# One kernel, its instruction groups issued in the order of a stored table instead of a greedy list

## The chip, the core and the metric

The kernel runs on one core of one Trainium2 chip. The core has a matrix engine (TensorE, "PE" in the profile; "PEld" is its loading of weights), VectorE (DVE), ScalarE (ACT), GpSimd (POOL), and SyncE (SP), which here issues all DMA transfers. Each engine works through its own list of instructions in order, and waits on semaphores for the others. The metric is the device time of one execution in microseconds.

## What is computed

A gated linear attention, whose state decays by alpha and takes in the product of k and v at each of 768 steps, for 4 batches of 8 heads of width 48. Its output, as a matrix of 768 by 384 for each batch, goes through a low-rank mix over the sequence and an MLP of width 1536 with a ReLU:

```python
def _attn_ref(q, k, v, alpha):
    B, H, S, D = q.shape                      # 4, 8, 768, 48
    state = np.zeros((B, H, D, D))
    for t in range(S):
        state = alpha[:, :, t, :, None] * state + np.einsum('bhd,bhe->bhde', k[:, :, t], v[:, :, t])
        y[:, :, t] = np.einsum('bhd,bhde->bhe', q[:, :, t], state)
    return y

def _moe_ref(x, U, V, w_ch1, w_ch2):          # x: (4, 768, 384)
    xt = x.transpose(0, 2, 1)
    h = xt @ U @ V                            # U: (768, 32), V: (32, 768)
    u = x + h.transpose(0, 2, 1)
    ch = np.maximum(u @ w_ch1, 0.0) @ w_ch2   # (384, 1536), (1536, 384)
    return u + ch
```

## The kernel before

The program is built from **groups**: a few instructions of one engine that are issued together, such as the four transposes of one tile. Each group is added to a plan with the tiles it reads and writes, the engines that may do it with an estimated cost in ns on each, a priority, and a mode (the tile shape that its matmuls use on TensorE: F is the full array; Q, R, C, V are others). A greedy list scheduler, run when the program is built, then orders them: again and again it takes the group that can start first by its estimates, with the priority to break ties, and gives it an engine and a buffer. What it decides is only an order for each engine and a choice of buffers; on the chip the semaphores decide when things run.

```python
class Plan:
    LAT = {"PE": 215.0, "ACT": 155.0, "DVE": 145.0, "POOL": 110.0, "SP": 200.0}
    SWITCH = 95.0
    TOL = 150.0
    EASE = 200.0
    STAY = 20.0
    # ...
    def run(self):
        # ... "ready" holds the groups whose inputs are planned
        while todo:
            per = {}
            for op in ready:
                t = op.est
                # ... t: not before a buffer is free (s[b.reserve])
                at = {eng: max(t, clock.get(eng, 0.0)) for eng in op.engs}
                soon = min(at[eng] + c for eng, c in op.engs.items()) + self.TOL
                for eng, c in op.engs.items():
                    if at[eng] + c <= soon:
                        per.setdefault(eng, []).append((at[eng], op))
            best = None
            for eng, ok in per.items():
                t0 = min(t for t, _ in ok)
                t1, op = min(((t, o) for t, o in ok if t <= t0 + 1.0), key=lambda x: (x[1].prio + (self.STAY if eng == "PE" and x[1].mode != mode else 0.0), x[1].i))
                key = (t1, t1 + op.engs[eng])
                if best is None or key < best[0]:
                    best = (key, eng, op)
            # ... takes a slot of each pool, moves the clocks of the engine and of the DMA
            done = end + self.LAT[eng]
            for b in op.bufs:
                b.left -= 1
                b.last = max(b.last, done + self.EASE)
                if b.left == 0:
                    b.pool.free[b.idx] = b.last
            for u in op.users:
                u.n -= 1
                if eng == "PE" and "PE" in u.engs:
                    u.est = max(u.est, end)
                else:
                    u.est = max(u.est, done + u.slack)
```

The constants that the groups need are made first, on VectorE and GpSimd, before the plan:

```python
    filler = const.tile([128, 512], BF16, name="filler")
    nc.vector.memset(filler, 0.0)
    # ... ones, onesel, offd: small, by memsets on VectorE
    for x in lt_s + rk_s:
        nc.vector.memset(x[:, :, D:], 0.0)
    rv2_s = slots("rw", 4, [C, 2, HP, 2, D], BF16)
    for x in rv2_s[:2]:
        nc.vector.memset(x, 0.0)
    ut_ones = const.tile([C, C], BF16, name="ut_ones")
    make_upper_triangular(nc, ut_ones, val=1.0, diag=True)
    ident = const.tile([C, C], BF16, name="ident")
    make_identity(nc, ident)
    upto = const.tile([C, C], BF16, name="upto")
    nc.vector.tensor_copy(upto, ut_ones)
    nc.vector.memset(upto[0:64, 64:128], 0.0)
    below = const.tile([C, C], BF16, name="below")
    nc.vector.tensor_tensor(below, upto, ident, op=ALU.subtract)
    mask2 = const.tile([C, 2, 2 * C], BF16, name="mask2")
    nc.gpsimd.memset(mask2, 0.0)
    nc.gpsimd.affine_select(
        out=mask2, in_=mask2, compare_op=ALU.is_gt, fill=1.0, base=0, pattern=[[1, 2], [-1, 2 * C]], channel_multiplier=2
    )
    maskp = const.tile([C, 1, 2, C], BF16, name="maskp")
    nc.vector.tensor_copy(maskp[0:64, 0], mask2[0:64, :, 0:C])
    nc.vector.tensor_copy(maskp[64:128, 0], mask2[64:128, :, C : 2 * C])
    maskc = const.tile([C, 1, C], BF16, name="maskc")
    for x in rq_s:
        nc.gpsimd.memset(x[:, :, D:], 0.0)
    for x in rv2_s[2:]:
        nc.gpsimd.memset(x, 0.0)
    nc.gpsimd.tensor_copy(maskc[:, 0, :], ut_ones)
    for g in range(4):
        nc.gpsimd.tensor_copy(sel[:, g, :], ident[0:R, 0:R])
```

The attention is done in units. Batches 0 and 1 have six units each: one is half of the heads over 256 steps, with two chunks of 64 in the halves of the partitions (`stage_pair`); batches 2 and 3 have units of all heads over 128 steps (`stage_gla`). A unit of the first kind, its groups in the order in which they are added (cut):

```python
        P.add({"ACT": 435}, lambda e: nc.scalar.activation(jh(lt()[:, :, 0:D]), raw(at), AF.Ln), r=[at], w=[lt], prio=pr + 40, slack=sl)
        # two groups: rv, v as bf16; POOL or ACT
        def f_cum(e):
            l2 = jh(lt()[:, :, 0:D])
            nc.tensor.matmul(cb()[:, 0:DM].rearrange("p (i h d) -> p i h d", i=2, d=D), lhsT=upto, rhs=l2[:, 0:1].to_broadcast([C, 2, HP, D]), start=True, stop=False)
            nc.tensor.matmul(cb()[:, 0:Q], lhsT=below, rhs=l2[:, 1], start=False, stop=False)
            nc.tensor.matmul(cb()[:, Q : 2 * Q], lhsT=upto, rhs=l2[:, 1], start=False, stop=False)
            # ... the unit's total decay: four narrow matmuls
        P.add({"PE": mm(DM, Q, Q, 8, 4, 4, 4, 4)}, f_cum, r=[lt], w=[cb], prio=pr + 30, slack=sl)
        aa, ai, tot = Buf(aas), Buf(ais), Buf(tots)
        P.add({"ACT": 390}, lambda e: nc.scalar.activation(ai().rearrange("t h d -> t (h d)"), cb()[:, 0:DM], AF.Exp, scale=-1.0), r=[cb], w=[ai], prio=pr + 20, slack=sl)
        P.add({"ACT": 390}, lambda e: nc.scalar.activation(aa().rearrange("t h d -> t (h d)"), cb()[:, 0:DM], AF.Exp), r=[cb], w=[aa], prio=pr + 21, slack=sl)
        P.add({"ACT": 100}, lambda e: nc.scalar.activation(tot()[:, :, 0], cb()[:, DM : DM + 8], AF.Exp), r=[cb], w=[tot], prio=pr + 22, slack=sl)
        both = {"DVE": 420, "POOL": 885}
        P.add(both, lambda e: f_scale(e, rk, kt, ai), r=[kt, ai], w=[rk], prio=pr + 10, slack=sl)
        P.add(both, lambda e: f_scale(e, rq, qt, aa), r=[qt, aa], w=[rq], prio=pr + 11, slack=sl)
        P.add({"PE": mm(*[C] * 4)}, lambda e: f_tr(rk, tk), r=[rk], w=[tk], prio=pr + 18, slack=sl)
        P.add({"PE": mm(*[C] * 4)}, lambda e: f_tr(rq, tq), r=[rq], w=[tq], prio=pr + 18, slack=sl)
        P.add({"DVE": 335, "ACT": 500}, lambda e: f_ev(e, kT, tk, False), r=[tk], w=[kT], prio=pr + 8, slack=sl)
        P.add({"DVE": 600, "ACT": 500}, lambda e: f_ev(e, qT, tq, True), r=[tq], w=[qT], prio=pr + 8, slack=sl)
        def f_sc(e):
            for n in range(4):
                a, j = n // 2, n % 2
                for par in range(2):
                    o = 64 * par
                    for c in range(2):
                        r = slice(64 * c, 64 * c + 64)
                        nc.tensor.matmul(
                            sc[par]()[r, n * C : (n + 1) * C],
                            lhsT=kT()[o : o + D, n, r], rhs=qT()[o : o + D, 2 * a + c, :],
                            start=(n == 0), stop=(n == 3), skip_group_check=True,
                        )

        P.add({"PE": mm(*[C] * 4)}, f_sc, r=[kT, qT], w=[sc[0], sc[1]], prio=pr + 10, mode="Q", slack=sl)
        def f_mask(par):
            s2 = sc[par]().rearrange("p (a j c) -> p a j c", a=2, j=2)
            dst = pm()[:, :, par, :].rearrange("p (a j) c -> p a j c", j=2)
            nc.vector.tensor_tensor(dst, s2, maskp.to_broadcast([C, 2, 2, C]), op=ALU.mult)

        for par in range(2):
            P.add({"DVE": 605}, lambda e, par=par: f_mask(par), r=[sc[par]], w=[(pm, par)], prio=pr + 5, slack=sl)
        # f_d (PE): k times v of the unit; f_st (DVE or POOL): the state, decayed; two chunks
        P.add({"PE": mm(*[2 * D] * 12)}, f_y, r=[qT, (rv, 0), (rv, 1), (pm, 0), (pm, 1)] + [x for x in before if x is not None], w=[yb], prio=pr, slack=sl)
        P.add(
            {"ACT": 385, "DVE": 460},
            lambda e: copy(e, xb()[:, 2 * blk : 2 * blk + 2, half * Q : (half + 1) * Q], yb()[:, 0 : 2 * Q].rearrange("p (c x) -> p c x", c=2)),
            r=[yb], w=[(xb, 2 * blk, half), (xb, 2 * blk + 1, half)], prio=pr, slack=sl,
        )
```

After the six units of a batch the low-rank mix needs all of them (`stage_mix`: utx, its copy, X and H matmuls into uT, copies on ScalarE or VectorE). Then come the two MLP layers, in two halves of the sequence and 12 blocks, and in six blocks of rows:

```python
    def mlp1(b, uT, h1, tt):
        for jt in range(NJ):
            hb = Buf(bank, RES[b])
            pr = mlp_prio(b, 0.25 * tt + jt * 0.02)
            # ...
            def f(e, jt=jt, hb=hb):
                for ct in range(NCT):
                    nc.tensor.matmul(
                        hb()[:, 0:TW], lhsT=w1_sb[:, ct, jt * 128 : (jt + 1) * 128],
                        rhs=uT()[:, ct, tt * TW : (tt + 1) * TW], start=(ct == 0), stop=(ct == NCT - 1),
                    )

            P.add({"PE": mm(TW, TW, TW)}, f, r=need + [("w1", jt // 3, ct) for ct in range(NCT)], w=[hb], prio=pr)
            # ... g: Relu on ScalarE, or max with 0 on VectorE
            P.add({"ACT": 395, "DVE": 470}, g, r=[hb], w=[(h1, tt, jt)], prio=-100)

    def mlp2(b, xb, ub, utx, h1, c):
        hb = Buf(bank, RES[b])
        tt = c // NT
        for g in range(3):   # four matmuls each, over 12 blocks of the hidden layer
            # ...
        ou = Buf(outs)
        P.add({"DVE": 468}, lambda e: nc.vector.tensor_tensor(ou(), (xb if b in XT else ub)()[:, c, :], hb()[:, 0:DM], op=ALU.add), r=[hb] + (xk(b, xb, c) if b in XT else [(ub, c)]), w=[ou], prio=-100)
        P.add({"SP": 550.0}, lambda e: nc.sync.dma_start(out[b, c * C : (c + 1) * C, :], ou()), r=[ou], prio=-1)
```

Where the plan leaves TensorE idle in the first 28 us, filler matmuls on a spare PSUM bank are put in[...].

Of the kernel before, what the change touches and what calls it, by code (L numbers as in the profile page):

```python
# [21 lines left out]
class Buf:  # L22


    def __init__(self, pool, reserve=0):
        self.pool = pool
        self.reserve = reserve
        self.slot = None
        self.idx = 0
        self.left = 0  # L30
        self.last = 0.0
# [5 lines left out]
class Op:  # L37
    __slots__ = ("engs", "fn", "prio", "deps", "bufs", "n", "users", "est", "i", "mode", "slack", "eng", "t")


class Plan:


    LAT = {"PE": 215.0, "ACT": 155.0, "DVE": 145.0, "POOL": 110.0, "SP": 200.0}
    SWITCH = 95.0
    TOL = 150.0
    EASE = 200.0
    STAY = 20.0
# [10 lines left out]
    def add(self, engs, fn, r=(), w=(), prio=0.0, mode="F", slack=0.0, after=()):  # L59
        op = Op()  # L60
        op.engs, op.fn, op.prio, op.mode, op.slack = engs, fn, prio, mode, slack
        op.i = len(self.ops)
        op.deps, op.users, op.est = set(), [], 0.0
# [14 lines left out]
        op.deps.update(x for x in after if x is not None)  # L78
# [12 lines left out]
    def run(self):  # L91
        for op in self.ops:
            op.n = len(op.deps)
            for d in op.deps:
                d.users.append(op)
        ready = [op for op in self.ops if op.n == 0]
        clock = {}
        order = []
        dma = 0.0
        mode = "F"  # L100
        todo = len(self.ops)
        while todo:
            per = {}
            for op in ready:
                t = op.est
                for b in op.bufs:
                    if b.slot is None:
                        s = sorted(x for x in b.pool.free if x is not None)
                        if len(s) <= b.reserve:
                            t = None  # L110
                            break
                        t = max(t, s[b.reserve])
                if t is None:
                    continue
                at = {eng: max(t, clock.get(eng, 0.0)) for eng in op.engs}
                soon = min(at[eng] + c for eng, c in op.engs.items()) + self.TOL
                for eng, c in op.engs.items():
                    if at[eng] + c <= soon:
                        per.setdefault(eng, []).append((at[eng], op))
            best = None  # L120
            for eng, ok in per.items():
                t0 = min(t for t, _ in ok)
                t1, op = min(((t, o) for t, o in ok if t <= t0 + 1.0), key=lambda x: (x[1].prio + (self.STAY if eng == "PE" and x[1].mode != mode else 0.0), x[1].i))
                key = (t1, t1 + op.engs[eng])
                if best is None or key < best[0]:
                    best = (key, eng, op)
            if best is None:
                raise RuntimeError("the plan is stuck")
            (t, _), eng, op = best
            for b in op.bufs:  # L130
                if b.slot is None:
                    p = b.pool
                    _, x = min((f, x) for x, f in enumerate(p.free) if f is not None)
                    p.free[x] = None
                    b.idx, b.slot = x, p.slots[x]
            ready.remove(op)
            op.eng, op.t = eng, t
            cost = op.engs[eng]
            if eng == "SP" and op.mode == "X":
                dma = max(dma, t) + cost  # L140
                clock[eng] = t + cost
                end = dma + 850.0
            elif eng == "SP":
                dma = max(dma, t + 600.0) + cost
                clock[eng] = max(t + 450.0, dma - 3500.0)
                end = dma + 2000.0
            else:
                if eng == "PE" and op.mode != mode:
                    cost += self.SWITCH
                    mode = op.mode  # L150
                clock[eng] = end = t + cost
            order.append(op)
            done = end + self.LAT[eng]
            for b in op.bufs:
                b.left -= 1
                b.last = max(b.last, done + self.EASE)
                if b.left == 0:
                    b.pool.free[b.idx] = b.last
            for u in op.users:
                u.n -= 1  # L160
                if eng == "PE" and "PE" in u.engs:
                    u.est = max(u.est, end)
                else:
                    u.est = max(u.est, done + u.slack)
                if u.n == 0:
                    ready.append(u)
            todo -= 1
        self.order = order
        self.clock = clock
        at = self.warm_from  # L170
        for op in order:
# [6 lines left out]
            op.fn(op.eng)  # L178

# [6 lines left out]
def kernel(  # L186
# [32 lines left out]
    W2AT = 7.9  # L219
    PAIR = (0, 1)  # L220
    TRD = {(3, c) for c in range(2, NC)}
    SL = 300.0
    TRU = (3,)
    XT = (0, 1)
    RES = (1, 1, 1, 0)
# [11 lines left out]
    nc.vector.memset(filler, 0.0)  # L237
# [15 lines left out]
    for x in lt_s + rk_s:  # L253
        nc.vector.memset(x[:, :, D:], 0.0)
    rv2_s = slots("rw", 4, [C, 2, HP, 2, D], BF16)
    for x in rv2_s[:2]:
        nc.vector.memset(x, 0.0)
    ut_ones = const.tile([C, C], BF16, name="ut_ones")
    make_upper_triangular(nc, ut_ones, val=1.0, diag=True)
    ident = const.tile([C, C], BF16, name="ident")  # L260
    make_identity(nc, ident)
    upto = const.tile([C, C], BF16, name="upto")
    nc.vector.tensor_copy(upto, ut_ones)
    nc.vector.memset(upto[0:64, 64:128], 0.0)
    below = const.tile([C, C], BF16, name="below")
    nc.vector.tensor_tensor(below, upto, ident, op=ALU.subtract)
    mask2 = const.tile([C, 2, 2 * C], BF16, name="mask2")
    nc.gpsimd.memset(mask2, 0.0)
    nc.gpsimd.affine_select(
        out=mask2, in_=mask2, compare_op=ALU.is_gt, fill=1.0, base=0, pattern=[[1, 2], [-1, 2 * C]], channel_multiplier=2  # L270
    )
    maskp = const.tile([C, 1, 2, C], BF16, name="maskp")
    nc.vector.tensor_copy(maskp[0:64, 0], mask2[0:64, :, 0:C])
    nc.vector.tensor_copy(maskp[64:128, 0], mask2[64:128, :, C : 2 * C])
    maskc = const.tile([C, 1, C], BF16, name="maskc")
    sel = const.tile([R, 4, R], BF16, name="sel")
    io = Pool(slots("io", 36, [C, H, D], FP32))
    for x in rq_s:
        nc.gpsimd.memset(x[:, :, D:], 0.0)
    for x in rv2_s[2:]:  # L280
        nc.gpsimd.memset(x, 0.0)
    nc.gpsimd.tensor_copy(maskc[:, 0, :], ut_ones)
    for g in range(4):
        nc.gpsimd.tensor_copy(sel[:, g, :], ident[0:R, 0:R])
# [35 lines left out]
    def small():  # L320
        P.add({"SP": 450.0}, lambda e: nc.sync.dma_start(u_in, moe_U.rearrange("(c p) r -> p c r", p=128)), w=["u_in"], prio=4.5)
        P.add({"SP": 500.0}, lambda e: nc.sync.dma_start(v_in, moe_V), w=["v_in"], prio=4.5)
        P.add({"POOL": 300}, lambda e: nc.gpsimd.tensor_copy(u_sb, u_in), r=["u_in"], w=["u"], prio=590)
        P.add({"POOL": 800}, lambda e: nc.gpsimd.tensor_copy(v_bf, v_in), r=["v_in"], w=["v_bf"], prio=591)
        for i in range(2):
            vb = Buf(bank)
            sl = slice(i * TW, (i + 1) * TW)
            P.add({"PE": mm(TW)}, lambda e, vb=vb, sl=sl: nc.tensor.matmul(vb()[:, 0:TW], lhsT=sel.rearrange("r a b -> r (a b)"), rhs=v_bf[:, sl], start=True, stop=True), r=["v_bf"], w=[vb], prio=592, mode="V")
            P.add({"DVE": 470, "ACT": 390}, lambda e, vb=vb, sl=sl: copy(e, vm_sb[:, sl], vb()[:, 0:TW]), r=[vb], w=[("vm", i)], prio=593)

    def weight(dst, src, key, prio, pr, engs):
        t = Buf(io)
        P.add({"SP": 590.0}, lambda e: nc.sync.dma_start(flat(t), src), w=[t], prio=prio)
        P.add(engs, lambda e: copy(e, dst, flat(t)), r=[t], w=[key], prio=pr)
# [4 lines left out]
    def weights1():  # L339
        for g in range(4):  # L340
            cs = slice(g * DM, (g + 1) * DM)
            for ct in range(NCT):
                weight(w1_sb[:, ct, cs], moe_w_ch1[ct * 128 : (ct + 1) * 128, cs], ("w1", g, ct), 5.5 + 0.01 * g, 560 + g, {"POOL": 485})

    def weights2():
        for jt in range(NJ):
            weight(w2_sb[:, jt, :], moe_w_ch2[jt * 128 : (jt + 1) * 128, :], ("w2", jt), W2AT + 0.001 * jt, 700 + jt, {"POOL": 485, "ACT": 435})

    LEAD = 4.0
    tiles = {}  # L350

    def stage_loads(b):
        def load(t, src, c, key):
            if b in PAIR:
# [6 lines left out]
                    w=[t], prio=key,  # L361
# [3 lines left out]
            P.add({"SP": 1080.0}, lambda e: nc.sync.dma_start(t(), src[b, :, sl, :].rearrange("h t d -> t h d")), w=[t], prio=key)  # L365

        for c in range(NC):
            at, qt, kt, vt = (Buf(io) for _ in range(4))
            tiles[b, c] = at, qt, kt, vt
            kk = b * NC + c  # L370
            for t, src, o in ((at, alpha, -0.7 if c else 0.0), (kt, k, 0.1), (qt, q, 0.2), (vt, v, 1.25 if c < NC - 1 and b in PAIR else 0.3)):
                load(t, src, c, kk + o)
# [502 lines left out]
```

## Time and profile before

| what | value |
|---|---|
| time, median of 3 runs | 170.48 us (170.03 to 170.65) |
| span of the profiled execution | 168.1 us |
| TensorE busy | 157.7 us, 94% |
| VectorE busy | 107.8 us, 64% |
| ScalarE busy | 101.6 us, 60% |
| GpSimd busy | 60.9 us, 36% |
| DMA | 30.44 MB, 181 GB/s in the mean |

The profile is one execution, recorded on the chip. The page gives each engine's busy time; then the span in 40 equal slices, where a digit is the busy share of a slice in tenths; then the chain of work that ended last, followed back from the last instruction. Other answers of the trace list what an engine did in order of time (start, length, engine, line, operation, output and inputs, count), or the busy time of each engine in a stretch that one asks for. "PE busy" counts overlapping matmuls, which are pipelined, so that a busy TensorE need not be at its peak. A line such as L787 is a line of the kernel.

### The profile page before, as it was taken

How to read it: one execution, taken by the hardware profiler on the slowest of the kernel's cores; microseconds unless marked ns; L12 is line 12 of the kernel's file. 1: busy time of each engine (PE TensorE's matmuls, PEld its weight loads, DVE VectorE, ACT ScalarE, POOL GpSimd, SP SyncE). 2: the span in 40 equal slices, each digit the busy share in tenths (PEclk: the TensorE clock that was granted, in tenths of full speed). 3: DMA queues.
4: the chain of work that ended last, by engine and by line, in shares of the span. 5: the costliest groups of instructions: out<-in, count | busy, mean ns of one | idle time of the engine just before them, and what ended most of it. 6: DMA issues, size and time to landing. Idle time of an engine off the chain costs nothing.

```text
span 168.1 us, 4500 instructions
## 1 busy us (share of the span) xinstructions
PE 157.7 (94%) x1693; PEld 102.7 (61%) x1698; DVE 107.8 (64%) x219; ACT 101.6 (60%) x237; POOL 60.9 (36%) x104
## 2 busy tenths in 40 slices
PE   7677797999999999999999999999999999999992
PEld 2355575566667777677666656666666566566660
DVE  7668886459969996689987679737644472001221
ACT  4489984799865744588898644247684102995000
POOL 8326389538311447476428361545400000000000
PEclk9999999999999999999999999999999999999999
DMA  5999999999999999899999999976130245200222
GB/s 137 271 261 262 247 324 330 273 294 336 274 244 265 174 226 223 189 195 219 189 170 201 193 195 229 181 184 143 37 62 0 86 118 151 72 4 0 94 94 94
DMA packets 89877, 30.44 MB, mean 181 GB/s; under 512 B 83680, under 2 KB 89824, under 8 KB 89856
## 3 DMA queue, kind: packets, MB, share of 16 engines
q1 hardware_dynamic: 89856, 30.16, 80.6%
q8 instruction: 13, 0.21, 0.6%
q14 instruction: 8, 0.07, 0.1%
HBM read 23.79 MB, written 4.72 MB: 170 GB/s over the span
## 4 chain that ended last, share of the span: by engine, by line
PE 83%; ACT 1%; DVE 0%; issue 0%; ACTq 0%
PE ps L787 28%; PE ps L812 28%; PE ps L633 2%; PE ps L612 2%; PE ps L440 2%; PE ps L548 2%; PE ps L467 2%; PE ps L692 1%; PE ps L574 1%; PE ps L731 1%; PE ps L709 1%; PE ps L740 1%; PE ps L817 1%; PE ps L499 1%; PE ps L656 1%; PE ps L690 1%
## 5 line engine op out<-in xcount | busy, mean ns | idle before, releaser
L812 PE MATMUL ps<-w_sb,h1t 128*128 128x384 bf16 x288 | 52.6, 326 | 0.0
L787 PE MATMUL ps<-uT,w_sb 128*128 128x384 bf16 x288 | 51.8, 326 | 0.0
L797 ACT ACTIVATE h1t<-ps 128x384 bf16<-128x384 f32 x71 | 34.7, 491 | 17.9 <-PE ps L787 17.8
L812 PEld LDWEIGHTS <-h1t 128*128 128x128 bf16 x288 | 26.5, 98 | 16.1 <-issue 0.5
L787 PEld LDWEIGHTS <-w_sb 128*128 128x128 bf16 x288 | 26.3, 98 | 15.8
L821 DVE TENSOR_TENSOR ou<-ub,ps 128x384 f32<-128x384 bf16 x12 | 6.7, 554 | 27.2 <-PE ps L812 27.2
L592 POOL TENSOR_TENSOR rk<-io,ai 128x384 bf16<-128x384 f32 x12 | 11.0, 914 | 26.7 <-ACT ai L585 26.7
L643 DVE TENSOR_TENSOR pm<-ps,maskc 128x512 bf16<-128x512 f32 x24 | 15.5, 683 | 4.5 <-PE ps L633 4.5
L799 DVE TENSOR_SCALAR h1t<-ps 128x384 bf16<-128x384 f32 x25 | 13.4, 552 | 5.5 <-PE ps L787 5.1
L478 DVE TENSOR_TENSOR pm<-ps,maskp 128x512 bf16<-128x512 f32 x24 | 15.5, 678 | 0.4 <-PE ps L467 0.3
L314 ACT CAST xb<-ps 128x384 bf16<-128x384 f32 x17 | 8.2, 480 | 7.9 <-PE ps L692 4.3
L314 ACT COPY kt<-ps 128x512 bf16<-128x512 bf16 x15 | 8.8, 583 | 5.6 <-PE ps L612 1.8
L318 POOL CAST w_sb<-io 128x384 bf16<-128x384 f32 x22 | 11.3, 549 | 1.4 <-DMA io<-in_moe_w_ch_dram 1.1
L592 POOL TENSOR_TENSOR rq<-io,aa 128x384 bf16<-128x384 f32 x12 | 11.0, 914 | 0.0
L821 DVE TENSOR_TENSOR ou<-xb,ps 128x384 f32<-128x384 bf16 x12 | 6.6, 550 | 6.7 <-PE ps L817 6.1
L318 POOL CAST rw<-io 64x384 bf16<-64x384 f32 x10 | 5.4, 545 | 11.7 <-DMA io<-in_v_dram 7.4
L420 ACT ACTIVATE ai<-ps 128x384 bf16<-128x384 f32 x12 | 5.9, 490 | 5.9 <-PE ps L413 5.7
L585 ACT ACTIVATE ai<-ps 128x384 bf16<-128x384 f32 x12 | 5.9, 493 | 5.5 <-PE ps L577 5.4
L307 PE MATMUL ps<-filler 128*128 128x512 bf16 x17 | 6.5, 477 | 1.6 <-DVE onesel L242 1.2
L314 ACT COPY qt<-ps 128x512 bf16<-128x512 bf16 x11 | 7.0, 640 | 1.5 <-PE ps L440 1.0
L391 ACT ACTIVATE lt<-io 128x384 bf16<-128x384 f32 x12 | 6.3, 525 | 1.5 <-DMA io<-in_alpha_dram 1.4
L314 ACT CAST rw<-io 64x384 bf16<-64x384 f32 x14 | 7.1, 508 | 0.1
(120 smaller groups left out, 263.9 us busy)
## 6 DMA issues: line engine op xcount, KB each, us to landing
io<-in_alpha_dram SPq DMA_DIRECT2D x24, 192.0 KB, 4.6
io<-in_k_dram SPq DMA_DIRECT2D x24, 192.0 KB, 4.4
io<-in_q_dram SPq DMA_DIRECT2D x24, 192.0 KB, 4.4
io<-in_v_dram SPq DMA_DIRECT2D x24, 192.0 KB, 4.4
io<-in_moe_w_ch_dram SPq DMA_DIRECT2D x24, 192.0 KB, 4.2
out_dram<-ou SPq DMA_DIRECT2D x24, 192.0 KB, 2.2
u_in<-in_moe_U_dram SPq DMA_DIRECT2D x1, 96.0 KB, 5.0
v_in<-in_moe_V_dram SPq DMA_DIRECT2D x1, 96.0 KB, 4.0
```

The source lines that it names most:

```text
L307: P.warm = lambda: nc.tensor.matmul(ps[:, 7, :], lhsT=filler[:, 0:128], rhs=filler, start=True, stop=True)
L314: nc.scalar.copy(dst, src)
L318: nc.gpsimd.tensor_copy(dst, src)
L391: P.add({"ACT": 435}, lambda e: nc.scalar.activation(jh(lt()[:, :, 0:D]), raw(at), AF.Ln), r=[at], w=[lt], prio=pr + 40, slack=sl)
L478: nc.vector.tensor_tensor(dst, s2, maskp.to_broadcast([C, 2, 2, C]), op=ALU.mult)
L592: eng.tensor_tensor(dst()[:, :, 0:D], a(), x(), op=ALU.mult)
L643: nc.vector.tensor_tensor(pm()[:, :, par, :], s2, maskc.to_broadcast([C, HP, C]), op=ALU.mult)
L787: nc.tensor.matmul(hb()[:, 0:TW], lhsT=w1_sb[:, ct, jt * 128 : (jt + 1) * 128], rhs=uT()[:, ct, tt * TW : (tt + 1) * TW], start=(ct == 0), ...
L797: nc.scalar.activation(dst, hb()[:, 0:TW], AF.Relu)
L799: nc.vector.tensor_scalar_max(dst, hb()[:, 0:TW], 0.0)
L812: nc.tensor.matmul(hb()[:, 0:DM], lhsT=h1()[:, jt, c * C : (c + 1) * C], rhs=w2_sb[:, jt, :], start=(jt == 0), stop=(jt == NJ - 1 and not ...
L821: P.add({"DVE": 468}, lambda e: nc.vector.tensor_tensor(ou(), (xb if b in XT else ub)()[:, c, :], hb()[:, 0:DM], op=ALU.add), r=[hb] + (xk ...
```

## The change

The scheduler goes. In its place stands a table of 1,039 entries, one for each group, in the order in which they are to be issued; the number is that of the group in the order in which groups are added to the plan, and a letter behind it names the engine where there is a choice (A ScalarE, V VectorE, G GpSimd). So 0 to 12 are the small constants and the low-rank weights, 13 to 60 the loads and casts of the MLP weights, 61 to 156 the loads of alpha, k, q and v of each unit in this order (61 alpha of unit 0 of batch 0, 67 q of unit 1), and 157 on the groups of the batches. The table was found by a long random search over durations that had been measured. Buffers are still taken by estimated times, now without the reserve and the allowances of the old plan, and the estimates know that VectorE and GpSimd share a port. No group is dropped. Five small copies on GpSimd (maskc and four of sel) become groups of the table.

The constants are made in another way: five tiles are cleared on VectorE, GpSimd fills triangles and a diagonal into three of them, and ScalarE copies two blocks of the triangles. The other clears all go to VectorE.

```diff
-    TOL = 150.0
-    EASE = 200.0
-    STAY = 20.0
+    PORT = 150.0
...
-    def run(self):
-        # the greedy scheduler
+    def place(self, table):
+
+        names = {"P": "PE", "A": "ACT", "V": "DVE", "G": "POOL", "S": "SP"}
...
+        for x in table.split():
+            op = self.ops[int(x.rstrip("PAVGS"))]
+            eng = op.eng = names[x[-1]] if x[-1] in names else next(iter(op.engs))
+            cost = op.engs[eng]
+            t = clock.get(eng, 0.0)
             for d in op.deps:
+                t = max(t, end[d] + (0.0 if eng == d.eng == "PE" else self.LAT[d.eng]))
...
+            if eng == "POOL":
+                t = max(t, port)
+            if eng == "DVE" and op.port:
+                t = max(t, port - self.PORT)
...
+    def run(self, table):
+        self.place(table)
...
+TABLE = """
+67 65 69 179 61 182 201 184 157 77 62 63 183 66 204 160 205 187G 247 189 161 162 207 64 68 191V 164V 166 186V 188 190A 185 168V 165V 73 71 167 192 70
+181G 180G 224 206 163 159G 169V 81 74 170 194 172 193 75 158G 209G 3 78 79 76 82 72 195 250 227 196 208V 83 173 211 210 251 228 268 229 197 213A 2 231G
+171 174 80 271 175 198 212V 214 273 274 272 84 85 176 89 232V 233 253 252 234 215 254G 6 5 199 177 255G 4 226G 275G 203G 15 31 33 35 236V 23 13 17 93
...
+816 821 811 954 960 957 830 969 965 817 822 967 963 961 977 968A 966V 971 983 984A 964A 962V 981 972V 978V 985 1005 831 991 975 1014 973 976V 1009 970V
+987 1006A 992V 974A 986A 988V 982V 1010 979 980A 832 995 989 990V 996A 1011 1007 993 999 1015 1016 1001 997 1012 1002V 994V 1000V 1017 1019 1003 1034
+1013 1020 812 1018 1021 1022 1029 1024 998A 1008A 1004A 1025 1026 1035 1030 1036 1027 1023 1028 827 1031 1037 1038 1032 1033
+"""
...
-    nc.vector.memset(filler, 0.0)
+    tri = const.tile([C, 2, C], BF16, name="tri")
+    ident = const.tile([C, C], BF16, name="ident")
+    blocks = const.tile([C, 2, C], BF16, name="blocks")
+    mask2 = const.tile([C, 2, 2 * C], BF16, name="mask2")
+    for x in (filler, tri, ident, mask2, blocks):
+        nc.vector.memset(x, 0.0)
+    nc.gpsimd.affine_select(
+        out=tri, in_=tri, compare_op=ALU.is_gt, fill=1.0, base=0, pattern=[[1, 2], [-1, C]], channel_multiplier=1
+    )
+    make_identity(nc, ident, nomemset=True)
+    nc.gpsimd.affine_select(
+        out=mask2, in_=mask2, compare_op=ALU.is_gt, fill=1.0, base=0, pattern=[[1, 2], [-1, 2 * C]], channel_multiplier=2
+    )
+    nc.scalar.copy(blocks[0:64, :, 0:64], tri[0:64, :, 0:64])
+    nc.scalar.copy(blocks[64:128, :, 64:128], tri[64:128, :, 64:128])
+    ut_ones, upto, below = tri[:, 0, :], blocks[:, 0, :], blocks[:, 1, :]
...
-    for x in lt_s + rk_s:
+    for x in lt_s + rk_s + rq_s:
         nc.vector.memset(x[:, :, D:], 0.0)
...
+    for x in rv2_s:
+        nc.vector.memset(x, 0.0)
...
+    P.add({"POOL": 250}, lambda e: nc.gpsimd.tensor_copy(maskc[:, 0, :], ut_ones), w=["maskc"])
+    for g in range(4):
+        P.add({"POOL": 150}, lambda e, g=g: nc.gpsimd.tensor_copy(sel[:, g, :], ident[0:R, 0:R]), w=[("sel", g)])
...
-            hb = Buf(bank, RES[b])
+            hb = Buf(bank)
...
-    P.run()
+    P.run(TABLE)
```

## The prediction

> **What bounds the kernel now.** I read the engine table and slices of the page first, then busy time by stage, then the timeline of TensorE and of VectorE.
>
> ```profile
> PE 157.7 (94%) x1693; PEld 102.7 (61%) x1698; DVE 107.8 (64%) x219; ACT 101.6 (60%) x237; POOL 60.9 (36%) x104
> ...
> PE   7677797999999999999999999999999999999992
> ...
> DVE  7668886459969996689987679737644472001221
> ACT  4489984799865744588898644247684102995000
> ...
> DMA  5999999999999999899999999976130245200222
> ...
> PE 83%; ACT 1%; DVE 0%; issue 0%; ACTq 0%
> ```
>
> Slice 8 onwards (a slice is 4.2 us) TensorE is full, and the chain that ended last is TensorE. Before that no engine is full, but the DMA is. So there are two regimes. The windows answer cut at the first MLP matmul (31.44 us) and at the end of TensorE's work (164.85 us) puts numbers on them; columns are window, length, then PE, PEld, DVE, ACT, POOL busy:
>
> ```profile
> 6.36:27.91 21.55, 17.13 (x294) 12.75 (x298) 17.24 (x34) 17.65 (x42) 11.34 (x17) 1.00 1.15 284
> ...
> 31.44:164.85 133.41, 133.37 (x1353) 86.42 (x1351) 84.83 (x161) 79.85 (x189) 41.01 (x60) 1.00 0.77 165
> ```
>
> Busy TensorE counts overlapping pipelined matmuls, so I asked what it really needs: the distance between starts in dense stretches. A 384-column matmul starts every 0.1625 us (11.70 us for the last 72 of line 787), a 128-column one every 0.056, a 96-column one every 0.042. Added up by line with the counts of the page, and leaving out the filler matmuls, the work is about 146 us: 93.6 for the 576 MLP matmuls, 9.8 for the 60 other full-width single ones, the rest for the small ones. Only 15.7 of the 146 lies before 31.44 us. In 31.44 to 164.85 (133.4 us) there are some 130 us of work with about 0.8 more in matmul records that are missing, so real bubbles are near 2.5 us. The sum is then: start of MLP 31.4 + later work 131 + bubbles 2.5 + the last VectorE add and store 3.25 = 168.1, the span.
>
> What is left to win is therefore (a) the head, 31.4 us for 15.7 us of work, and (b) the 2.5 us of bubbles. Most of (b) is one thing. The tile-shape changes of TensorE:
>
> ```profile
> 68.96 0.82 PE L812 MATMUL ps<-w_sb,h1t 128*128 128x384 bf16 x4
> 69.72 0.40 PE L633 MATMUL ps<-qt,kt 48*128 48x128 bf16 x8
> 70.05 0.82 PE L812 MATMUL ps<-w_sb,h1t 128*128 128x384 bf16 x4
> ```
>
> Four full-width matmuls need 0.65 us but the score group starts 0.76 after them: 0.11 lost. It then holds TensorE for 0.33, where four steps of 0.056 (two heads run side by side in the rows) need 0.22: another 0.11. A lone score group costs 0.2 us of change, 0.1 in and 0.1 out. My work sum has the second half inside it.
>
> **What the skill says.** The Trainium skill, TensorEngine Tiling (Array Packing), Key Properties: changing the tiling mode drains TensorE. The trace agrees, 0.1 us a change. SBUF — State Buffer, SBUF: two separate sides: VectorE and GpSimd hold their shared port pair exclusively for a whole instruction. The trace agrees: the 128x128 copy into upto took 1.76 us under GpSimd memsets where the 64x256 mask copies after them took 0.23, and it delayed the first real matmul. TensorE: Matmul & The Clock Gate, Architectural detail: VectorE and ScalarE are strict FIFOs, so a badly placed table entry blocks all behind it; the trace has no such case of size to check it on.
>
> **The change, part by part.**
>
> 1. Work removed: none on TensorE or the DMA. All groups are there, 1,039 entries; only their order, engine and buffers change. So 146 us of matmul stays, and no gain is possible beyond (a) and (b).
>
> 2. Setup. Upto and below now come from two ScalarE copies of a select on GpSimd instead of VectorE's 1.76 us copy, memset and subtract. Before, Ln ended at 3.92 but the first real matmul was at 5.03, held by upto. Now the mask should be ready by about 2.7 (estimate: the activation table load ends at 2.01, then two ScalarE copies of 64x128, some 0.3 each, between the 0.19 of a 128x8 Exp and the 0.51 of a 64x384 cast), so Ln is the limit. But I number the groups in the order in which they are added: the table's loads begin q(0,1), alpha(0,1), alpha(0,2), alpha(0,0), alpha(0,4), k(0,0). Alpha is second, issued 0.5 us later, so Ln ends near 4.45, cumsum 4.55 to 5.0, and the ScalarE row of the table has a second Ln before the first Exp. That Exp runs near 5.4 to 5.9, then a GpSimd product (0.91), a transpose (0.4), and only then VectorE's first entry, the q copy, at about 7.2. Before, VectorE's first product began at 6.36. The setup gain is given back by the deeper pipelining here.
>
> 3. The head. VectorE's table entries up to the last mask of batch 0, by their measured durations: 12 masks x 0.64 = 7.7; 10 states x 0.343 = 3.4; q copies 3 x 0.69 = 2.1; k copies 3 x 0.424 = 1.3; products 3 x 0.66 + 3 x 0.70 = 4.1. Sum 18.6 us. ScalarE's up to the copy of the low-rank product: 8 Ln x 0.525, 14 Exp x 0.49, 7 small Exp x 0.19, 3 k copies x 0.585, 3 q copies x 0.735, 3 casts of v x 0.51, 6 other copies x 0.49 = 20.8 us from 3.95 us on, so it could end at 24.7; VectorE binds. From 7.2 without idle: 25.8. Before, VectorE was busy 17.24 of 21.55 us there, idle 20%; all alphas load early now and four or five units run interleaved, so I give it 1 us idle, less 0.4 because the table's own times mind the port shared with GpSimd (a product took 0.56 when it met no GpSimd work, 0.66 to 0.70 in the mean): 26.4, against 27.91. From last mask to first MLP matmul took 3.5 us before (y, copy, low-rank product, copy, uT copy) and is the same chain: 29.9 against 31.44, so 1.5 us. The table also puts the cumsums of units (1,0) and (1,1) ahead of that point: 2 x 0.45 us more work done by then, of which I count 0.5. Head: -2.0 us. Loads of batch 0 are 24 as before but U and V go behind them; the DMA delivers batch 0 about 1.5 us earlier, so it allows this.
>
> 4. Tile-shape changes. Counting in the trace: 60 changes before, 16 of them in the head. In the table: 37, 13 of them before the first MLP group; score groups of two or three units now stand side by side. After the head 44 become 24: 20 x 0.1 = -2.0 us, all on TensorE's path.
>
> 5. New stalls. The old list left 0.3 us slack per group and 0.2 us before a buffer's reuse; the table has neither, and MLP groups of both halves and of two layers are mixed. I put +0.5. The last two stores now issue 0.65 us apart (the last two adds follow one matmul group apart) where they were 1.95 apart: +0.2 at the end for a store that queues. Other bubbles (0.5) stay.
>
> Sum: -2.0 - 2.0 + 0.5 + 0.2 = -3.3, from 170.48 to 167.2. Here I choose: my 1 us of VectorE idle in the head is a guess, and a long search over measured durations should have squeezed it further, so I take 0.6 more: -3.9, **166.6 us**.
>
> **Rivals.** A, the head doesn't move: the DMA is full from 4 us to 110 us and the strict order of VectorE waits on GpSimd products (0.91 each, 12 products of which 6 are there). For: DMA digits of 9, and item 2's later start. Then only the changes of tile shape pay: 168.7 or so. B, the order is too tight: a wait in one FIFO blocks others, TensorE gets bubbles of 0.3 us at twenty places in 31 to 165 us, which eats all: 170 to 172. For: no slack left. Against: VectorE and ScalarE are at 64% and 60% there, so they catch up. C, the search found a head with VectorE full from 6 us: MLP starts at 28 us: 164.5. For: VectorE was idle 4.3 us in the head. Against: the start computed in 2.
>
> **Range and chances.** The middle is the sum above. Rival C gives the low end, 164.4; A with part of B the high end, 169.0. 2% faster means under 167.07, so the middle lies just beyond it: faster 0.55, within 0.41, slower 0.04 (needs B in full and more).
>
> **What would show it.** First MLP matmul near 30 us (31.44 before); first VectorE work of a unit near 7 us; about 24 shape changes after it; span of line 787 and 812 groups unchanged at 0.1625 us a matmul; TensorE idle under 3 us from there to its last matmul, near 161 us; last store 3.3 us behind it. I am wrong if the first MLP matmul comes at 31 us or later, or if waits of TensorE on relu copies or on PSUM banks add up to more than 1.5 us after it.

## The result and the profile after

| | before | changed |
|---|---|---|
| median time | 170.56 us | 165.08 us (164.71 to 165.65, 4 runs) |
| ratio | | 0.969 (95%: 0.965 to 0.972) |
| span of the profiled execution | 168.1 us | 162.8 us |
| first MLP matmul starts | 31.44 us | 29.36 us |
| from there to the last matmul's end | 133.4 us | 130.15 us |
| last matmul's end to the end of the span | 3.3 us | 3.3 us |

The 5.3 us of the span fall into 2.1 us in the head and 3.2 us in the stretch in which TensorE is full. From the page of the changed kernel, first each engine's busy time and share, then the slices (4.07 us each):

```profile
PE 154.6 (95%) x1691; PEld 102.8 (63%) x1691; DVE 111.1 (68%) x240; ACT 87.9 (54%) x214; POOL 66.2 (41%) x106
...
PE   7878789999999999999999999999999999999991
...
DVE  6389997536756989765579677896689465562512
...
DMA  5999999999999999997998995995757133402124
```

TensorE is at 90% or more from the seventh slice on (24.4 us) where it was from the eighth (29.4 us). The work is the same (fillers left out, both traces have the same 1,676 matmuls), but ScalarE has 13.7 us less to do (101.6 to 87.9 us), and VectorE and GpSimd more: the table lets VectorE do 50 of the 96 ReLU groups where it did 25.

The busy times by stage; columns are window, length, then PE, PEld, DVE, ACT and POOL busy. The first window runs from VectorE's first work on a unit to the end of the last mask of batch 0, the second is the full stretch of TensorE:

```profile
7.88:25.80 17.92, 14.97 (x272) 11.17 (x271) 17.22 (x35) 12.41 (x34) 11.34 (x21) 1.00 1.17 267
29.36:159.51 130.15, 130.15 (x1338) 86.08 (x1335) 87.44 (x173) 67.44 (x164) 49.75 (x72) 1.00 0.78 174
```

The head's gain is in the first line: VectorE has the same 17.2 us of work there as before, but does it in 17.9 us instead of 21.55. It starts 1.5 us later (7.88 against 6.36) and ends 2.1 us earlier (25.8 against 27.9).

In the full stretch, the score groups changed most: these are the matmuls of q with k, on 48 rows of the array, so that the tile shape changes ahead of them and behind. Timeline of TensorE; columns are start, length, engine, line, operation, count:

```profile
83.27 0.81 PE L798 MATMUL ps<-w_sb,h1t 128*128 128x384 bf16 x4
84.01 0.84 PE L625 MATMUL ps<-qt,kt 48*128 48x128 bf16 x24
84.79 0.82 PE L798 MATMUL ps<-w_sb,h1t 128*128 128x384 bf16 x4
```

Three score groups stand side by side: 0.78 us for what took 3 x 0.33 us as lone groups, besides 0.1 us ahead of each. In the trace the tile shape changes 24 times after the first MLP matmul, where it changed 44 times. No wait of TensorE in that stretch is long enough to be listed, before or after.

### The profile page after: what moved, and what is told of

Read it like the earlier page. It is cut to its first block, busy times and chain, and to the rows that moved or that the text cites. A ratio compares the mean times of both kernels' runs of the same rounds, so it can differ in the third digit from the quotient of the medians.

```text
span 162.8 us, 4450 instructions
## 1 busy us (share of the span) xinstructions
PE 154.6 (95%) x1691; PEld 102.8 (63%) x1691; DVE 111.1 (68%) x240; ACT 87.9 (54%) x214; POOL 66.2 (41%) x106
## 4 chain that ended last, share of the span: by engine, by line
PE 86%; DVE 6%; DMA 3%; SPq 2%; issue 1%
PE ps L798 29%; PE ps L773 29%; DMA io<-in_k_dram 3%; PE ps L435 3%; PE ps L543 2%; DVE pm L473 2%; SPq L356 2%; PE ps L604 2%; PE ps L625 2%; DVE rq L422 2%; PE ps L684 1%; PE ps L718 1%; PE ps L494 1%; PE ps L462 1%; PE ps L566 1%
## 5 line engine op out<-in xcount | busy, mean ns | idle before, releaser
L798 PE MATMUL ps<-w_sb,h1t 128*128 128x384 bf16 x288 | 54.2, 326 | 0.0
L783 ACT ACTIVATE h1t<-ps 128x384 bf16<-128x384 f32 x46 | 21.4, 496 | 35.4 <-PE ps L773 35.1
L785 DVE TENSOR_SCALAR h1t<-ps 128x384 bf16<-128x384 f32 x50 | 25.8, 552 | 21.0 <-PE ps L773 20.9
L798 PEld LDWEIGHTS <-h1t 128*128 128x128 bf16 x288 | 26.4, 97 | 16.4 <-issue 0.6
L584 POOL TENSOR_TENSOR rk<-io,ai 128x384 bf16<-128x384 f32 x12 | 11.0, 915 | 10.0 <-PE ps L773 3.9
L584 POOL TENSOR_TENSOR rq<-io,aa 128x384 bf16<-128x384 f32 x12 | 11.0, 927 | 2.2 <-ACT aa L578 1.2
L317 POOL CAST rv<-io 128x384 bf16<-128x384 f32 x12 | 6.0, 503 | 9.6 <-DMA io<-in_v_dram 9.6
L317 POOL CAST w_sb<-io 128x384 bf16<-128x384 f32 x16 | 7.7, 507 | 4.7 <-DMA io<-in_moe_w_ch_dram 4.7
L315 DVE COPY qt<-ps 128x512 bf16<-128x512 bf16 x9 | 5.6, 627 | 4.6 <-PE ps L435 3.5
L659 POOL TENSOR_TENSOR st<-sm,tot 128x384 bf16<-128x384 f32 x6 | 5.0, 831 | 9.1 <-DVE sm L671 9.1
L422 POOL TENSOR_TENSOR rk<-io,ai 128x384 bf16<-128x384 f32 x8 | 7.3, 912 | 3.3 <-DMA io<-in_k_dram 1.4
L422 POOL TENSOR_TENSOR rq<-io,aa 128x384 bf16<-128x384 f32 x7 | 6.4, 913 | 5.3 <-ACT aa L416 5.3
L731 DVE TENSOR_TENSOR ub<-xb,ps 128x384 bf16<-128x384 bf16 x12 | 6.0, 550 | 3.3 <-PE ps L730 3.3
```

The lines of the kernel that those rows point to most:

```text
L317: nc.gpsimd.tensor_copy(dst, src)
L422: eng.tensor_tensor(jh(dst()[:, :, 0:D]), raw(a), jh(x()), op=ALU.mult)
L584: eng.tensor_tensor(dst()[:, :, 0:D], a(), x(), op=ALU.mult)
L731: P.add({"DVE": 465}, lambda e, c=c, hb=hb: nc.vector.tensor_tensor(ub()[:, c, :], xb()[:, c, :], hb()[:, 0:DM], op=ALU.add), r=[hb] + xk( ...
L783: nc.scalar.activation(dst, hb()[:, 0:TW], AF.Relu)
L785: nc.vector.tensor_scalar_max(dst, hb()[:, 0:TW], 0.0)
```

## The experiments

Every kernel below is the changed kernel with one thing altered. "Old order" is what the greedy list of the kernel before decided, with its engines, in the numbers of the table. "Start" is the first MLP matmul, "head" what comes before it, "rest" the time from there to the last matmul's end; start and rest are from one execution, the profiled one. The ratio is to the kernel before, run beside it. A cumsum is the group of matmuls that adds up the logarithms (Ln) of a unit's alphas.

| kernel | median us | ratio (95%) | start | rest | shape changes in the rest |
|---|---|---|---|---|---|
| changed | 165.08 | 0.969 (0.965 to 0.972) | 29.36 | 130.15 | 24 |
| old order | 169.16 | 0.993 (0.991 to 0.995) | 30.82 | 133.20 | 44 |
| new head, old rest, first cut | 172.93 | 1.017 (1.013 to 1.021) | 30.14 | 137.43 | 44 |
| old head, new rest, first cut | 169.86 | 0.999 (0.997 to 1.001) | 33.76 | 131.82 | 24 |
| new head, old rest, mended | 168.57 | 0.990 (0.988 to 0.993) | 29.23 | 133.96 | 44 |
| old head, new rest, mended | 167.88 | 0.986 (0.983 to 0.988) | 32.46 | 130.28 | 24 |
| new head and batch 1's Ln, old rest | 168.95 | 0.990 (0.988 to 0.993) | 29.56 | 134.72 | 44 |
| scattered scores | 168.52 | 0.988 (0.985 to 0.992) | 29.14 | 134.49 | 41 |
| split bundles | 166.59 | 0.980 (0.977 to 0.982) | 29.20 | 131.92 | 40 |
| touch ahead | 165.13 | 0.970 (0.968 to 0.972) | 29.64 | 130.23 | 24 |
| alpha first | 165.03 | 0.967 (0.965 to 0.969) | 29.27 | 130.28 | 24 |
| alpha first, Exp earlier | 165.29 | 0.969 (0.966 to 0.971) | 29.04 | 130.22 | 24 |
| old setup | 164.65 | 0.969 (0.965 to 0.972) | 29.25 | 130.14 | 24 |

A part of each time lies outside the profiled span: 1.7 to 1.8 us in old order, old setup, scattered, the mended old head with new rest, and the run with batch 1's Ln ahead; 2.1 us in the other kernels with a table; 2.0 us in the kernel before. So a difference of 0.4 us between two medians need not come from the order, and the spans (median of the executions) are given where that matters.

### The order or the setup

```diff
 TABLE = """
-67 65 69 179 61 182 201 184 157 77 62 63 183 66 204 160 205 187G ...
+0 1 2 3 4 61 62 63 65 66 67 64 69 157 70 160 71 161 68 162 164V ...
```

> The changed kernel, but its table holds the old list's order, group for group and engine for engine (the five small GpSimd copies come first). So only the new way of making the masks and the new choice of buffers are left of the change. Theory (the order is the gain): the masks come earlier, the first matmul is then held by Ln alone at about 4.5 us instead of 5.03, and a part of that is lost again in the chain of VectorE: 170.0 to 170.5. Rival (the setup is a good part of the gain): 168.5 or less, MLP start at 30 us or before.

The measured 169.16 lies between the two expectations: 1.2 us by the ratio (0.7% of 170.5), and 1.1 us by the spans (168.5 to 167.4). The trace shows about half of it in the head: the first real matmul runs at 4.14 us instead of 5.03, and the MLP starts 0.62 us earlier. The rest is 0.2 us shorter. This run has the new setup and the new choice of buffers; the two were not tested apart, so 1.2 us is what they bring together. What is left, 169.16 - 165.08 = 4.1 us, is the table's order with its engines; these two weren't tested apart either. The counterpart puts the old setup under the table:

```diff
-    for x in (filler, tri, ident, mask2, blocks):
-        nc.vector.memset(x, 0.0)
-    # ... select into tri and mask2, two ScalarE copies into blocks
+    nc.vector.memset(filler, 0.0)
+    make_upper_triangular(nc, ut_ones, val=1.0, diag=True)
+    # ... ident, upto, below, mask2, maskp and the clears as in the kernel before
```

> The changed kernel with its table, but the masks and the clears made as in the kernel before (the triangle copied and cut on VectorE, three clears on GpSimd); the copies of maskc and sel stay in the table. Theory (the table loads q first, so Ln ends at 4.8 us anyway and the first matmul at 5.0 us waits for Ln, not for the masks; upto is ready at about 5.0): the setup is worth 0 to 0.3 us here, 165.0 to 165.5. Rival (the new setup is worth as much as under the old order, where it brought 1.2 us): 166.1 to 166.5.

It costs nothing: 0.969 either way, and the spans are 162.85 and 162.95 us. Its timeline shows why (DVE is VectorE, ACT ScalarE; what ended an engine's idle time stands in brackets):

```profile
3.06 1.76 DVE L265 COPY upto<-ut_ones 128x128 bf16<-128x128 bf16 x1
...
4.26 0.52 ACT L389 ACTIVATE lt<-io 128x384 bf16<-128x384 f32 x1 [2.25 <-DMA io<-in_alpha_dram]
...
5.03 0.34 PE L404 MATMUL ps<-lt,upto 128*128 128x384 bf16 x1
```

The slow copy is back and upto is ready just before 5.03 us; but the table's first alpha is the second load, Ln ends at 4.78, and with the new setup the first matmul ran at 4.89 us. The new masks are early for nothing here: 0.14 us at the first matmul, 0.3 us at VectorE's first copy (8.18 against 7.88 us), none at the last mask of batch 0 (25.67 against 25.80) or the start of the MLP.

### Head and rest, one without the other

Both halves were put together at the first MLP matmul of either list. The cuts of this section give the rule; the edit itself is the table's text.

```diff
+# head: the list up to its first MLP matmul; rest: the other list without these groups
+order = head(new) + [g for g in old if g not in head(new)]     # new head, old rest
+order = head(old) + [g for g in new if g not in head(old)]     # old head, new rest
```

> The table's order up to the first MLP matmul of batch 0, then the old list's order for all that is left. Theory (two gains that add up): the head brings its own 2.1 us and the 0.9 us of the two cumsums done ahead, the old order after it keeps its 44 shape changes: 167.3 to 168.2. Rival A (the start of the MLP doesn't count, TensorE would only wait later for loads): 170 or more. Rival B (all of the gain is in the head): 165.5.

> The old order up to the first MLP matmul, then the table's. Theory: the MLP starts at about 31 us, after it the shape changes fall from 44 to 24, about 2.2 us: 167.8 to 168.7. Rival B (all in the head): 170.3. Rival C (all in the order after it): 165.5.

Both expectations failed (172.93 and 169.86 us). The cut itself is at fault, as the mended cut below confirms: the table's list runs ahead with loads of batch 1 and of the second layer's weights, so that each half waited for loads or casts which the other half had put elsewhere. With the old rest, TensorE waited 0.9 us just ahead of the start and 4.5 us in all after it, the longest times for a product of VectorE (1.8) and for a weight cast (1.3). With the new rest it waited 1.9 us ahead of the start for the Ln of batch 1.

The rest of 131.82 us in the second run is not to be compared with the others. From its page the granted clock (in tenths, a slice is 4.2 us), and from its timeline the wait for an Ln and the MLP's first matmuls:

```profile
PEclk9999999959999999999999999999999999999999
...
33.31 0.32 PE L401 MATMUL ps<-lt,blocks 128*128 128x384 bf16 x1 [1.11 <-ACT lt L386]
...
33.76 2.67 PE L773 MATMUL ps<-uT,w_sb 128*128 128x384 bf16 x8
```

The clock was 0.51 in the mean from 33.8 to 37.3 us, and the eight matmuls took 2.67 us, where eight with starts 0.1625 us apart take 1.46; by the distances of the starts this cost the rest 1.6 us. Of the 22 executions 7, this one among them, took 171.0 us or more with a mean clock of 0.99, the other 15 took 169.4 to 170.3 us.

So the cut was mended: the head is only what the first MLP matmul needs of batch 0 itself.

```diff
-# head: the list up to its first MLP matmul
+# head: the 189 groups of batch 0 that its uT copies depend on, and the low-rank weights
```

> The seam mended: only what the first MLP matmul needs of batch 0 itself (attention, low-rank mix, their loads: 189 groups) stands in the table's order, all else, with the loads of the MLP weights, in the old list's order behind it. Theory: the MLP starts at about 29.4 us instead of the 30.8 of the run with the old order, TensorE then goes on as in that run (133.2 us), so 1.4 us less than its 169.2: 167.5 to 168.1. Rival A (an earlier start only means later waits): 169 or more.

> The other half with the same seam: the 189 groups in the old order, all else in the table's. Theory: the MLP starts at 30.8 us, then 24 shape changes instead of 44 and no other waits; the two cumsums of batch 1 can't run ahead (0.9 us): 130.15 + 0.9 us after the start, 166.9 to 167.6. Rival (what made the rest better is tied to the new head): 168.5 or more.

Both times lie between theory and rival. Alone, the new head wins 0.3% over the old order (0.990 against 0.993, with intervals that overlap) and the new rest 0.7% (0.986); together they win 2.4%. By the spans it is 0.95, 1.3 and 4.45 us. So they don't add up. Yet each half won its own part in full: against the old order (30.82 and 133.20) the new head starts the MLP 1.6 us earlier, and the new rest is 2.9 us shorter. What was lost lies on the other side of the seam, 0.8 us in the old rest and 1.6 us in the old head, and the trace names the waits. With the old head and the new rest, the table's TensorE list puts two cumsums of batch 1 ahead of the MLP, and their Ln now stands behind the uT copies of the old head:

```profile
30.45 0.33 PE L722 MATMUL ps<-vm_sb,utx 128*128 128x384 bf16 x1
...
31.55 0.32 PE L402 MATMUL ps<-lt,blocks 128*128 128x384 bf16 x1 [0.77 <-ACT lt L387]
...
32.46 0.97 PE L774 MATMUL ps<-uT,w_sb 128*128 128x384 bf16 x5
```

The uT of this run would have allowed the MLP at about 30.6 us; it began at 32.46, because TensorE takes its list in order. With the new head and the old rest, the start came at 29.23 as expected but the rest took 0.8 us longer than with the old head, 0.59 us of it a wait of a cumsum for batch 1's Ln. Was that all that was missing? The eleven groups of batch 1 that the table runs ahead were put ahead there too:

```diff
+head = head + [alpha loads, Ln, cumsums, Exps of units (1,0) and (1,1)]
```

> As the mended run with the new head and the old rest, but the eleven groups of batch 1 that the table puts ahead of the MLP on TensorE and ScalarE (two loads of alpha, two Ln, two cumsums, five Exp) stand ahead here too. Theory (what was missing at the seam was batch 1's Ln and cumsum): the MLP starts at 29.4 us, TensorE then needs 133.2 - 0.9 us, 166.7 to 167.5, against 168.6 without them. Rival (the old rest doesn't fit the new head for another cause): 168.2 to 168.8.

It wasn't: 168.95, just above the rival's range. The rest grew to 134.72 us although 0.9 us of it had been done ahead. From the list of TensorE's waits (who waits, for whom, us in total, times, longest), in the rest of this run:

```profile
PE ps L495 <- POOL rw L318: 1.3, 1, 1.3
PE ps L649 <- POOL rk L585: 0.3, 1, 0.3
```

and the timeline at that wait:

```profile
36.88 0.50 POOL L318 CAST rw<-io 64x384 bf16<-64x384 f32 x1 [3.19 <-DMA io<-in_v_dram]
...
37.43 0.49 PE L495 MATMUL ps<-rw,rk 128*128 128x192 bf16 x4 [1.34 <-POOL rw L318]
```

GpSimd's cast waited 3.19 us for v of batch 1, and TensorE for the cast. The same two in the run of the old order:

```profile
36.22 0.54 POOL L318 CAST rw<-io 64x384 bf16<-64x384 f32 x1 [5.25 <-DMA io<-in_v_dram]
...
38.02 0.49 PE L495 MATMUL ps<-rw,rk 128*128 128x192 bf16 x4
```

There TensorE came to the product 1.8 us after the cast's start; here it was through with the work ahead of it at 35.9 us, before the cast. So an earlier MLP brings the old list sooner to groups whose loads haven't come. The table has 51 matmuls of the first layer ahead of its first transpose of batch 1 (38.11 us), the old list 33 (34.92 us here). The old rest was 133.20 behind the old head; 134.72 + 0.9 is 2.4 more. At the two waits the next start comes 2.0 us late; the other 0.4 us stay open. The profiled execution was the slowest of the six (169.57 us).

### What a shape change costs

In the first try, score groups that stand side by side were pulled apart by moving the later ones behind one or two full-shape groups; where three stood together, the last two also changed places.

```diff
-(TensorE's list; sc: scores of a batch and unit, cum: cumsum, M: MLP) ... sc2.3 sc2.1 sc2.2 M2 cum2.4 M1 ...
+(TensorE's list) ... sc2.3 M2 sc2.2 cum2.4 sc2.1 M1 ...
```

> The table, but where two or three score groups stand side by side on TensorE after the head, they are pulled apart by one or two full-shape groups each; 12 groups move by a place or a few, nothing else. Shape changes after the head: 41 instead of 24. Theory (0.11 us a change, all on the path): 17 x 0.11 = 1.9 us more, 166.7 to 167.2. Rival (the changes are small print, the order gains by fewer waits): 165.1 to 165.6.

3.4 us, above both numbers: moving scores also delays their masks. The trace lists 0.8 us of waits of TensorE (a mask 0.4, a weight cast 0.2, a ReLU 0.2). Added up from start to start of the matmuls, 2.4 of the 4.3 us in the rest lie at the score groups and shape changes, and 1.6 at six places elsewhere. A cleaner test leaves each group where it is:

```diff
+            # before a score group that follows another one on TensorE (eight of them):
+            nc.tensor.matmul(sc[0]()[:, 0:2], lhsT=filler[:, 0:128], rhs=filler[:, 0:2], start=True, stop=True)
```

> The changed kernel with eight two-column full-shape matmuls added, each between two score groups that stand side by side after the head; they write into the bank that the next score group overwrites. No group moves. Shape changes after the head: 40 instead of 24. Theory (0.11 us a change, all of it on TensorE's path): 16 x 0.11 + 8 x 0.025 = 2.0 us more, 166.8 to 167.3. Rival (the loss of 3.4 us of the scattered run came from scores that were late, not from changes): 165.1 to 165.7.

```diff
+            # the same eight, ahead of the first score group of each bundle
```

> The control to the run with split bundles: the same eight two-column matmuls, but all of a bundle's ahead of its first score group, where TensorE is in full shape anyway. 24 shape changes, as in the changed kernel. Both theories: 8 x 0.025 = 0.2 us more, 165.1 to 165.5.

166.59 against 165.13: 1.46 us for 16 changes, 0.09 us each, a little below the theory, and the eight matmuls themselves cost nothing that shows. By the rest of the two traces it is 131.92 - 130.23 = 1.69 us, 0.11 us each. The same three score groups as above, split:

```profile
83.80 0.81 PE L811 MATMUL ps<-w_sb,h1t 128*128 128x384 bf16 x4
84.55 0.40 PE L638 MATMUL ps<-qt,kt 48*128 48x128 bf16 x8
84.88 0.18 PE L634 MATMUL ps<-filler 128*128 128x2 bf16 x1
84.99 0.40 PE L638 MATMUL ps<-qt,kt 48*128 48x128 bf16 x8
85.32 0.18 PE L634 MATMUL ps<-filler 128*128 128x2 bf16 x1
85.43 0.40 PE L638 MATMUL ps<-qt,kt 48*128 48x128 bf16 x8
85.75 0.82 PE L811 MATMUL ps<-w_sb,h1t 128*128 128x384 bf16 x4
```

From the first score to the next full-shape work it takes 85.75 - 84.55 = 1.20 us instead of 0.78: 0.42 us for four more changes and two narrow matmuls.

### Can the head start earlier still?

The loads of q and of alpha of unit 1 changed places; then, on top of that, the first Exp went ahead of the Ln of the third load.

```diff
-67 65 69 179 61 182 201 184 157
+65 67 69 179 61 182 201 184 157
```

> The changed kernel with its first two table entries exchanged: alpha of unit 1 is loaded first, its q second. Theory: Ln starts at 3.4 us instead of 4.29, but the first Exp stands behind the Ln of the third load in ScalarE's list, which waits for that load until 5.5 us as before, so VectorE still starts near 7.9 us and nothing comes of it: 164.9 to 165.3. Rival (the second place of alpha costs its 0.5 us or more): 164.5 or less.

```diff
-65 67 69 179 61 182 201 184 157
+65 67 69 179 61 182 184 201 157
```

> As alpha first, and the first Exp stands ahead of the Ln of the third load in ScalarE's list. Theory: the first Exp at 4.7 us, VectorE's first copy at 6.6 instead of 7.9 us, but the products that follow wait for the fourth and later loads as before, so only the 0.7 us of that copy can be won at the start and some of it is lost again: the MLP starts at 28.8 to 29.2 us, 164.5 to 165.0. Rival (VectorE's start sets the head in full): 1.3 us, 163.8.

Neither can be told from the changed kernel by its time (the start of 29.04 in the second is from one of its two fastest executions, 164.69 us). The first went as the theory said at the end, though VectorE did start at 7.60; the last mask ended at 25.70, as in the changed kernel (25.80). The second kept VectorE's first copy at 7.88 us, against my 6.6. The first Exp did come early (5.15 us, not 4.7; the cumsum ahead of it took 0.9 us, at a granted clock of 0.5), but the transpose of the product behind it stands on TensorE after the cumsums of the third and fourth loads:

```profile
7.36 0.24 PE L409 MATMUL ps<-onesel,lt 128*128 128x4 bf16 x4
7.46 0.38 PE L436 MATMUL ps<-ident,rq 128*128 128x128 bf16 x4
```

TensorE's list held it back, as ScalarE's had held the Exp. One entry moved in one list meets the next list.

## Why the prediction was right

**The end of the sum.** 166.6 us were foretold, 165.08 came. The two mechanisms were the right ones; the sum of -3.3, made -3.9 by choice, is short of the measured -5.5.

**The head (step 3).** Start of the MLP 29.9 foretold, 29.36 measured. VectorE nearly fills its window, as foretold; its work was counted 8% too high (18.6 us against 17.2 in the trace). Its first work on a unit came later than the 7.2 us I worked out (7.88). Its idle time was 17.92 - 17.22 = 0.7 us where I had put 1 us, less 0.4. So the last mask, foretold for 26.4, ended at 25.8. From last mask to MLP 3.5 us foretold, 3.6 measured. But the window does not simply move with VectorE's start: with starts of 7.60 and 8.18 us (alpha first, old setup) the last mask ended at 25.70 and 25.67. VectorE was idle for 1.1 and 0.6 us there.

**Cumsums ahead (step 3).** I counted 0.5 of 0.9 us. They ran before the start, so the rest is shorter by all of it.

**Shape changes (step 4).** 44 to 24, counted in the table, is what the trace has (in the head it has 15, where 13 were counted). 20 x 0.1 was foretold; by the split bundles it is 20 x 0.09 = 1.8 us from the times and 2.1 us from the traces.

**New stalls (step 5).** This term failed: +0.5 foretold, none measured. The rest is 3.2 us shorter. The distances from each matmul's start to the next, added up over the rest in both traces, account for it: 0.9 us less for the cumsums, 2.1 us less at the score groups and the other shape changes (8.6 to 6.5 us), and 0.2 us less spread over all else, whose cause stays open. No wait of TensorE is listed there; VectorE is idle for 33% of that stretch and ScalarE for 48%, but whether that is why the missing allowances did no harm was not tested.

**The bubbles.** The 2.5 us were too few. 0.8 us of the stretch was put down to missing matmul records, but in the trace before only fillers lack records (22 weight loads, 17 matmuls), all of them in the head. With 0.22 us needed for each of the 24 score groups, the 8.6 and 6.5 us above hold 3.3 us lost at shape changes before, and 1.2 us after.

**The last stores (step 5).** +0.2 foretold, nothing measured: 3.3 us from the last matmul to the end in both.

**Setup (step 2).** Right for the changed kernel: given back by the order in which the table loads. What I didn't see is that under the old order it is worth up to 1.2 us, together with the new choice of buffers.

**The rivals.** A, that the DMA holds the head, is refuted for the table; when the old rest followed the new head, loads of batch 1 that came late took back 0.8 of the 1.6 us. B, too tight an order, is refuted for this table, but waits of that kind stand in all five hybrids. C (start at 28 us) went too far, by the start as worked out in step 2.

## What to carry to other kernels

Where one engine is full, count its work from the distances between starts, and what is left to win is the time before it is full, plus what its own sequence costs; here 20 changes of tile shape at about 0.1 us each could be counted in the table ahead of the run. A half of one order put together with a half of another can lose at the seam a good part of what it wins: here one half alone was worth 0.3%, the other 0.7%, both 2.4%, since TensorE came there to matmuls whose loads or Ln the other list had put later. And before speeding up one engine's first step, follow it through the lists of the others, for the next strict list may hold it at the same time as before.

## What was not expected

Eight extra matmuls of two columns on the full TensorE did not show in the time (165.13 against 165.08 us) as long as they changed no tile shape, but cost 1.46 us when they did.
